# The last block of W_q for two groups, as two blocks of 64 rows on partitions 0 to 63

## The chip, the cores and the metric

The kernel runs on one core of a Trainium2 chip. The metric is the device time of one execution in microseconds (us). Before the change the median of three runs is 735.13 us (734.92 to 736.19). The engines that matter here are TensorE (PE, with its weight loads PEld), VectorE (DVE), ScalarE (ACT), and SyncE (SP), whose queue issues nearly all loads from HBM to on-chip memory. The loads run on the core's 16 DMA engines.

## The reference

Four layers follow each other: attention A, gated MLP B, A again, B again, each with a residual sum, and both A layers use the same weights and caches, as both B layers do. There is one token for each of four batches, `x` of 4 x 640.

```
x = x + A(layernorm(x))          # twice, each followed by
x = x + B(layernorm(x))

A:  q = x @ wq                   # 640 x 4096, 32 heads of 128
    k, v = the last 1024 positions of the caches, for each batch and head
    o = softmax(q k^T / sqrt(128)) v
    out = o @ wo                 # 4096 x 640
B:  gate = x @ W_gate; up = x @ W_up      # 640 x 1728 each
    out = (gate * (gate > 0) * up) @ W_down
```

All values are float32. For four tokens nearly all the work is to bring weights and caches in: each pair of a head and a layer has 4 MB of K and V.

## The kernel before, in words

Nothing is kept of the matrices from one layer to the next, except for the last five heads (the groups `K0` of three and `K1` of two, the row `kept`), whose data stay on chip from layer 0 to layer 1. All else is loaded again.

**Rows in HBM.** The host lays the data out in rows of 128 partitions: `heads` (27 heads in six groups of four and one of three, with their W_q, K, V and W_o in the order in which they are used), `kept` (the same of the last five heads) and `mlp`. A load copies a range of columns of such a row, on all 128 partitions, to a range of columns of `store`, a ring-like buffer of 53,120 columns of four bytes on each partition. One load of 13,312 columns is 6,656 KB.

**W_q.** W_q has 640 rows, which are five blocks (`KC`) of 128 rows. For a group of four heads a block is 512 columns. Its part `q` in the row `heads` is 2,560 columns, five times 512.

**The order of the loads.** `plan` (lines 113 to 191) is a list written at build time: which range of which row goes to which columns of `store`. `put` appends loads cut at given columns, `stretch` (line 124) fills `store` up to its quarters (`QUARTERS`), wraps to column 0 and goes on. `load` (line 196) is called whenever a range of `store` has been used for the last time (`done`, line 220): it takes loads from the plan, in order, for as long as the target columns of the next are free, and issues each with one `nc.sync.dma_start` (line 204) on SP's queue. SP executes them in order; a load whose target is still in use waits on SP, and all later ones wait behind it.

**The compute.** `normalized` (line 289) makes the layer norm, and turns the 640 values of the four tokens into `xT`: on 128 partitions, four columns for each of the five blocks (line 308). `query` (line 329) multiplies blocks 0 to 3 on four column groups of the array into `qp` (line 336), and block 4 on top of the first (line 343), then `query_turned` transposes. `scores` (line 360) multiplies K (line 367), `softmax` and `turned` follow, `values` (line 382) multiplies V (line 395), `project` multiplies W_o (line 425) into the sum `y`. `forward` is the MLP. In `attention` (line 429) these are interleaved over the groups: the query of a group is made two groups ahead, its scores one ahead.

**What sets the order around the change.** The loads go through SP's queue in plan order. The compute waits for each load as a whole: a matmul that needs one column of a load waits until all of that load has landed.

Each load raises a semaphore when it has landed. In the trace all loads use the same eight semaphores (99, 101, 102, 103 and 106 to 109), in turn.

Of the kernel before, what the change touches and what calls it, by code (L numbers as in the profile page):

```python
# [7 lines left out]
F32 = mybir.dt.float32  # L8
# [4 lines left out]
B, D, H, DH, W, F = 4, 640, 32, 128, 1024, 1728  # L13
P = 128
KC = D // P
# [10 lines left out]
KV = 4096  # L26
HEADS = [list(range(h, h + 4)) for h in range(0, 24, 4)] + [[24, 25, 26], [27, 28, 29], [30, 31]]
SIDE = 4
N = len(HEADS)
K0, K1 = N - 2, N - 1  # L30
KEPT = len(HEADS[K0]) + len(HEADS[K1])


def of(what, g):
    return [(what, h) for h in HEADS[g]]


def step(g):
# [5 lines left out]
PARTS = {  # L44
    "heads": [("q", 0), ("q", 1), *of("k", 0)] + [p for g in range(K0) for p in step(g)] + of("o", K0 - 1),
    "kept": [*of("o", K0), *of("o", K1), ("q", K0), ("q", K1), *of("k", K0), *of("k", K1), *of("v", K0), *of("v", K1)],
}


# [12 lines left out]
SPARE = 768  # L62
QUARTERS = [STORE // 4, STORE // 2, STORE // 4 * 3, STORE]
FRONT = KEPT * 2 * (D + KV)
FIRST, MOST = 6976, 16320


def size_of(what, i):
    return len(HEADS[i]) * D if what == "q" else D if what == "o" else KV


def spread(parts):


    at, places, cuts = 0, {}, [0]
    for what, i in parts:
        places[what, i] = at
        size = size_of(what, i)
        step = {"q": size // KC, "k": 512, "v": 512, "o": D}[what]
        cuts += range(at + step, at + size + 1, step)  # L80
        at += size
    return places, at, cuts
# [11 lines left out]
def decode_kernel(ctx: ExitStack, tc: tile.TileContext, x, source, sel, out):  # L94
    nc = tc.nc
    const = ctx.enter_context(tc.tile_pool(name="const", bufs=1))
# [3 lines left out]
    ps_p = ctx.enter_context(tc.tile_pool(name="ps_p", bufs=2, space=bass.MemoryType.PSUM))  # L100
# [5 lines left out]
    store = big.tile([P, STORE], F32, name="store")  # L106
# [8 lines left out]
    def put(layer, row, to, *cuts):  # L115

        for lo, hi in zip(cuts, cuts[1:]):
            assert hi - lo <= MOST and to % 64 == 0 and lo in known[row] and hi in known[row], (row, lo, hi)
            assert to + hi - lo <= (STORE if to < STORE else STORE + SPARE), (row, lo, hi, to)
            plan.append((layer, row, lo, hi, to))  # L120
            to += hi - lo
        return to

    def stretch(layer, lo, end, to, goals):

        while lo < end:
            room = min([g - to for g in goals if g - to >= 2048] or [0])
            hi = max(c for c in ROWS["heads"][2] if c <= min(end, lo + room))
            if hi > lo:
                to = put(layer, "heads", to, lo, hi)  # L130
                lo = hi
            else:
                to = 0
        return to

    def at_part(what, i):
        return WHERE[what, i][1]

    def near(c, row="heads"):

        return max(x for x in ROWS[row][2] if x <= c)
# [37 lines left out]
        lo = hi  # L179
    hi = near(lo + 5120)  # L180
    to = put(1, "heads", to, lo, hi)
    lo, hi = hi, near(hi + STORE - to)
    put(1, "heads", to, lo, hi)
    v = at_part("v", HEADS[K0 - 1][-1])
    to = stretch(1, hi, near(v - 8192), 0, QUARTERS)
    to = put(1, "heads", to, near(v - 8192), heads_end)
    cuts = [0, 7040, 12160, GU0 + 3 * GU, WD1 + WD, MLP - 4 * D, MLP - 2 * D, MLP - D, MLP]
    for lo, hi in zip(cuts, cuts[1:]):
        to = put(1, "mlp", to if to + hi - lo <= STORE else 0, lo, hi)
# [6 lines left out]
    def load():  # L196

        if not held:
            nc.sync.dma_start(out=first_q, in_=source["heads"][:, :HELD])
        while plan and not any(live[plan[-1][4]:plan[-1][4] + plan[-1][3] - plan[-1][2]]):  # L200
            layer, row, lo, hi, to = plan.pop()
            live[to:to + hi - lo] = [True] * (hi - lo)
            held.setdefault((layer, row), []).append((lo, hi - lo, to))
            nc.sync.dma_start(out=place(to, hi - lo), in_=source[row][:, lo:hi])

    def place(to, n):
        return store[:, to:to + n] if to < STORE else probs[:, W - SPARE - 48 + to - STORE:][:, :n]
# [22 lines left out]
    def part(layer, what, h, lo, n):  # L230

        row, first = WHERE[what, h]
        return get(layer, row, first + lo, n)

    def part_done(layer, what, h, lo, n):
        row, first = WHERE[what, h]
        done(layer, row, first + lo, n)
# [6 lines left out]
    nc.scalar.dma_start(out=sel_sb, in_=sel)  # L244


    xT = const.tile([P, KC * B + 28], F32, name="xT")


    qT = const.tile([P, SIDE - 1 + SIDE * SIDE * B], F32, name="qT")  # L250
# [35 lines left out]
            nc.tensor.matmul(m[32 * g:32 * g + 32], sel_q, a, start=True, stop=True, tile_position=(0, 32 * g))  # L286
        return m

    def normalized():

        ysb, xc, sq = probs[:, :QUARTER], gates[:, :QUARTER], gates[:, QUARTER:2 * QUARTER]
        waits[0] = True
        su = small.tile([P, 1], F32, name="su", bufs=1)
        nc.vector.tensor_reduce(su, y, axis=AX.X, op=ALU.add)
        nc.scalar.copy(ysb, y)
        busy(2)
        mu = mean(su, "mu")
        nc.vector.tensor_tensor(xc, ysb, mu.to_broadcast([P, QUARTER]), op=ALU.subtract)
        ss = small.tile([P, 1], F32, name="ss", bufs=1)
        nc.scalar.activation(sq, xc, AF.Square, accum_out=ss)  # L300
        busy(1)

        pt = ps_p.tile([P, KC, 32], F32, tag="p", name="xt_ps")
        nc.tensor.transpose(pt[:, :4], xc[:, :P], ident)
        for g in range(4):
            nc.tensor.matmul(pt[32 * g:32 * g + 32, 4, :B], xc[:, P:], ident[:, 32 * g:32 * g + B],
                             start=True, stop=True, tile_position=(0, 32 * g))
        nc.vector.tensor_copy(xT[:, :KC * B].rearrange("p (c b) -> p c b", b=B), pt[:, :, :B])
        return ss

    def deviation(ss):
        var = mean(ss, "var")
        rs = small.tile([P, 1], F32, name="rstd")
        nc.scalar.activation(rs, var, AF.Sqrt, bias=eps_sb)
        nc.vector.reciprocal(rs, rs)
        return rs
# [12 lines left out]
    def query(layer, g, spread=False):  # L329


        n = len(HEADS[g]) * P
        qp[g] = ps_m.tile([P, n], F32, tag="m", name="qp")
        for c in range(KC - 1):
            for a, b in [(0, HELD - c * n), (HELD - c * n, n)] if g == 0 and c * n < HELD < c * n + n else [(0, n)]:
                nc.tensor.matmul(qp[g][32 * c:32 * c + 32, a:b], xT[:, B * c:B * c + 32],  # L336
                                 part(layer, "q", g, c * n + a, b - a),
                                 start=True, stop=c > 0 and not spread or b < n, tile_position=(0, 32 * c))
        part_done(layer, "q", g, 0, (KC - 1) * n)
        c = KC - 1  # L340
        m = n // 4 if spread else n
        for a in range(n // m):
            nc.tensor.matmul(qp[g][32 * a:32 * a + 32, a * m:a * m + m], xT[:, B * c:B * c + 32],  # L343
                             part(layer, "q", g, c * n + a * m, m), start=False, stop=True, tile_position=(0, 32 * a))
        part_done(layer, "q", g, c * n, n)
# [82 lines left out]

    def attention(layer):
        gs = order[layer]  # L430
        rstd = deviation(normalized())
        table(AF.Exp)
        query(layer, gs[0], True)
        query_out(gs[0], rstd)
        query(layer, gs[1])
        query_turned(gs[0])
        go_on()
        query_out(gs[1], rstd)
        scores(layer, gs[0])
        query(layer, gs[2])  # L440
        softmax(gs[0])
        query_turned(gs[1])
        query_out(gs[2], rstd)
        for before, g, after, then in zip([None] + gs, gs, gs[1:] + [None], gs[2:] + [None] * 2):
            totals(g)
            turned(g)
            if layer == 0 and after is None:
                live[STORE:] = [False] * SPARE
                load()
            if before is not None:  # L450
                values_turned(before)
            if then is not None and before is not None:
                query(layer, then)
                query_out(then, rstd)
            if after is not None:
                scores(layer, after)
                softmax(after)
            else:
                table(AF.Sqrt)
            if then is not None:  # L460
                query_turned(then)

            if before is not None and not (layer == 0 and after is None):
                project(layer, before)
            values(layer, g, after is None)
        values_turned(gs[-1])
        if layer == 0:
            project(layer, gs[-2])
        project(layer, gs[-1], True)
# [134 lines left out]
```

## Time and profile before

| | us |
|---|---|
| median of three runs | 735.13 |
| lowest and highest | 734.92, 736.19 |
| the profiled execution | 734.91 |
| its span, from the first to the last instruction | 733.0 |
| PE busy in the span | 448.8 (61%) |
| DVE busy | 75.3 (10%) |
| ACT busy | 47.1 (6%) |
| bytes read from HBM | 311.85 MB, 426 GB/s over the span |

The profiled execution lies 0.22 us under the median. The mean granted TensorE clock is 0.82. A profile shows each engine's instructions, the DMA queues and what ended each wait. A share of the DMA is a mean over the core's 16 DMA engines: at 1.00 all sixteen move data all the time.

### The profile page before, as it was taken

Reading aid. Unit: us, or ns where it says so; the run is one execution under the profiler, and the core shown is the slowest. Engines: PE = TensorE matmul, PEld = TensorE weight load, DVE = VectorE, ACT = ScalarE, POOL = GpSimd, SP = SyncE. Lnnn points to the kernel's source line nnn. Section 1 sums busy time; section 2 is a strip of 40 time slices with the busy share of each in tenths; the row PEclk is TensorE's granted clock in tenths of the full one; section 3 lists DMA queues with packets and bytes.
Section 4 is the critical chain, followed back from the end, with each engine's and each line's share of the span. In section 5 each row is a group of like instructions: output and inputs, shape, how many; then the busy total and the mean of one; then the engine's idle time right before and its main releaser. Section 6 shows DMA issues by size and latency. Waiting matters only on the chain.

```text
span 733.0 us, 8209 instructions
## 1 busy us (share of the span) xinstructions
PE 448.8 (61%) x3739; PEld 139.2 (19%) x3739; DVE 75.3 (10%) x279; ACT 47.1 (6%) x88; POOL 0.2 (0%) x4
## 2 busy tenths in 40 slices
PE   0666566746457634529778896546666457555576
PEld 0211111111112111203333231101111012111133
DVE  1111000010000101002101221001010010101011
ACT  0200000000000000001201110000000000000100
POOL 0000000000000000000000000000000000000000
PEclk9988868978868767759999999776878778779779
DMA  9999999999999999999999999999999999999996
GB/s 391 447 432 419 436 445 419 446 419 438 440 418 454 422 434 433 427 426 428 419 401 413 432 432 449 434 433 425 443 424 443 433 425 447 428 429 433 423 424 285
DMA packets 14010, 312.45 MB, mean 426 GB/s; under 512 B 1556, under 2 KB 1812, under 8 KB 7192
## 3 DMA queue, kind: packets, MB, share of 16 engines
q1 hardware_dynamic: 13824, 311.84, 99.0%
q8 instruction: 29, 0.48, 0.2%
q10 hardware_dynamic: 152, 0.09, 0.0%
q14 instruction: 5, 0.04, 0.0%
HBM read 311.85 MB, written 0.08 MB: 426 GB/s over the span
## 4 chain that ended last, share of the span: by engine, by line
DMA 55%; PE 29%; another core or an unknown queue 14%; DVE 1%; issue 1%; ACT 0%; SPq 0%; DVEq 0%; ACTq 0%
DMA store<-in_heads 39%; PE ps L367 13%; PE po L395 9%; DMA store<-in_kept 9%; DMA store<-in_mlp 7%; PE y L425 2%; PE pp L380 1%; PE qp L336 1%; PE gu L482 1%; PE qp L343 1%; PE qt L355 1%; DVE nm L371 0%; PE ot L415 0%; ACT probs L375 0%
## 5 line engine op out<-in xcount | busy, mean ns | idle before, releaser
L367 PE MATMUL ps<-store,qT 128*4 128x512 f32 x1024 | 166.2, 715 | 119.8 <-DMA store<-in_heads 98.1
L395 PE MATMUL po<-store,pT 128*16 128x512 f32 x1024 | 154.3, 726 | 99.3 <-DMA store<-in_heads 93.5
L367 PEld LDWEIGHTS ps<-store,qT 128*4 128x4 f32 x1024 | 30.1, 95 | 236.2 <-DMA store<-in_heads 113.9
L395 PEld LDWEIGHTS po<-store,pT 128*16 128x16 f32 x1024 | 32.9, 111 | 206.4 <-issue 123.8
L371 DVE TENSOR_REDUCE nm<-ps 128x1 f32<-128x1024 f32 x18 | 22.0, 1225 | 266.4 <-PE ps L367 266.4
L375 ACT ACTIVATE probs<-ps,nm 128x1024 f32<-128x1024 f32 x18 | 20.1, 1114 | 346.8 <-DVE nm L371 338.7
L425 PE MATMUL y<-store,oT 128*4 128x160 f32 x512 | 24.7, 324 | 17.6 <-DMA store<-in_heads 16.0
L391 DVE COPY pT<-pp 128x16 f32<-128x16 f32 x128 | 17.2, 169 | 141.4 <-PE po L395 141.4
L482 PE MATMUL gu<-store,xT 128*32 128x256 f32 (+1 forms) x288 | 21.5, 362 | 5.5 <-DMA store<-in_mlp 4.8
L402 ACT COPY gates<-po 128x512 f32<-128x512 f32 x16 | 9.4, 587 | 234.8 <-PE po L395 234.8
L336 PE MATMUL qp<-store,xT 128*32 128x512 f32 (+2 forms) x130 | 21.1, 607 | 4.8 <-DMA store<-in_heads 4.7
L380 PE MATMUL pp<-sel_sb,probs 128*128 128x128 f32 x144 | 19.5, 281 | 0.0
L425 PEld LDWEIGHTS y<-store,oT 128*4 128x4 f32 x512 | 12.9, 91 | 27.4 <-DMA store<-in_heads 16.7
L380 PEld LDWEIGHTS pp<-sel_sb,probs 128*128 128x128 f32 x144 | 17.1, 145 | 0.0
L408 DVE RECIPROCAL r<-so 128x16 f32<-128x16 f32 x18 | 4.6, 258 | 112.7 <-PE so L406 112.7
L343 PE MATMUL qp<-store,xT 128*32 128x512 f32 (+4 forms) x46 | 16.1, 498 | 0.0
L270 PE MATMUL y<-probs,sel_sb 4*4 4x160 f32 x8 | 0.7, 445 | 24.9 <-DMA sel_sb<-in_sel 24.9
L348 DVE TENSOR_SCALAR gates<-qp,rstd 128x512 f32<-128x512 f32 (+2 forms) x18 | 12.4, 690 | 23.2 <-PE qp L343 20.3
L355 PE MATMUL qt<-sel_sb,gates 128*128 128x128 f32 x64 | 12.8, 325 | 0.0
L482 PEld LDWEIGHTS gu<-store,xT 128*32 128x32 f32 x288 | 10.0, 109 | 14.5 <-DMA store<-in_mlp 9.0
L513 PE MATMUL y<-store,hT 128*4 128x160 f32 x192 | 9.6, 299 | 4.6 <-DMA store<-in_mlp 4.5
L415 PE MATMUL ot<-sel_sb,gates 128*128 128x128 f32 x72 | 11.5, 279 | 1.2 <-DVE gates L399 1.2
(70 smaller groups left out, 113.8 us busy)
## 6 DMA issues: line engine op xcount, KB each, us to landing
store<-in_heads SPq DMA_DIRECT2D x15, 6656.0 KB, 53.1
store<-in_heads SPq DMA_DIRECT2D x5, 6400.0 KB, 51.6
store<-in_heads SPq DMA_DIRECT2D x2, 6848.0 KB, 48.6
store<-in_heads SPq DMA_DIRECT2D x2, 6592.0 KB, 49.5
store<-in_heads SPq DMA_DIRECT2D x2, 6464.0 KB, 48.5
store<-in_mlp SPq DMA_DIRECT2D x15, 640.0 KB, 6.9
store<-in_kept SPq DMA_DIRECT2D x2, 4096.0 KB, 43.7
store<-in_heads SPq DMA_DIRECT2D x1, 8064.0 KB, 23.4
```

Source lines behind the costliest of these rows:

```text
L336: nc.tensor.matmul(qp[g][32 * c:32 * c + 32, a:b], xT[:, B * c:B * c + 32], part(layer, "q", g, c * n + a, b - a), start=True, stop=c > 0 ...
L343: nc.tensor.matmul(qp[g][32 * a:32 * a + 32, a * m:a * m + m], xT[:, B * c:B * c + 32], part(layer, "q", g, c * n + a * m, m), start=False ...
L348: nc.vector.tensor_scalar(gates[:, :len(HEADS[g]) * P], qp.pop(g), rstd, SCALE, op0=ALU.mult, op1=ALU.mult)
L355: nc.tensor.transpose(qt[:, i], gates[:, i * P:(i + 1) * P], ident)
L367: nc.tensor.matmul(ps[32 * b:32 * b + SIDE, j, :], qT[:, at:at + SIDE], part(layer, "k", h, lo, 512), start=i == 0, stop=i == n - 1, tile_ ...
L371: nc.vector.tensor_reduce(nm[g], ps.rearrange("p j n -> p (j n)"), axis=AX.X, op=ALU.max, negate=True)
L375: nc.scalar.activation(probs, ps.rearrange("p j n -> p (j n)"), AF.Exp, bias=nm.pop(g), accum_out=sums[g])
L380: nc.tensor.transpose(pps[g][c // 4][:, c % 4, :], probs[:, c * P:(c + 1) * P], ident)
L391: nc.vector.tensor_copy(to[:, 4 * j:4 * j + 4], pp[j][:, :, i:P:32])
L395: nc.tensor.matmul(po[32 * a:32 * a + SIDE * B, :], t[:, at:at + SIDE * B], part(layer, "v", h, c * 512, 512), start=i == 0 and c < 4, sto ...
L425: nc.tensor.matmul(y[32 * a:32 * a + B], o[:, i], part(layer, "o", h, a * QUARTER, QUARTER), start=False, stop=last and h == HEADS[g][-1], ...
L482: nc.tensor.matmul(gus[j][32 * g:32 * g + 32, :2 * n], xT[:, B * c:B * c + 32], get(layer, "mlp", lo, 2 * n), start=c == 0, stop=c == KC - ...
```

## The change

For two of the six common groups, 3 and 4, the part `q` has four blocks of 128 rows (2,048 columns) instead of five. The fifth block, 128 rows by 512 columns, goes to a new row `half`: its first 64 rows and its last 64 rows lie side by side on partitions 0 to 63, 1,024 columns wide. The row `half` has 64 rows in HBM.

- **Loads.** A `half` part is fetched by eight loads in a loop, one for each `p` in 0, 1, 2, 3, 32, 33, 34, 35: eight rows `p, p+4, ..., p+28`, 4,096 bytes each, 32 KB for a load. In `store` the part takes 1,024 columns on all partitions as far as the plan's book-keeping goes.
- **Plan.** `stretch` inserts the `half` part of a group ahead of the load that holds the start of the group's `q`. In layer 1 there is also a `put` of columns 0 to 1,024 of the row, which is group 3's part, behind the load of 5,120 columns. `FIRST` falls by 1,024, and the last load of `heads` in layer 1 begins 640 columns earlier by its goal.
- **Compute.** `normalized` has two more small matmuls and a copy in the attention layers: they put the second half of the fifth block's values on partitions 0 to 63, in four more columns of `xT`. `query` multiplies the two half blocks with two matmuls of 64 rows instead of one of 128.

```diff
+HALF = 3, 4
...
-FIRST, MOST = 6976, 16320
+FIRST, MOST = 5952, 16320
...
+        todo = [g for g in HALF if lo <= at_part("q", g) < end]
         while lo < end:
             room = min([g - to for g in goals if g - to >= 2048] or [0])
             hi = max(c for c in ROWS["heads"][2] if c <= min(end, lo + room))
-            if hi > lo:
+            if todo and at_part("q", todo[0]) < hi:
+                a = at_part("half", todo.pop(0))
+                to = put(layer, "half", to, a, a + 1024)
+            elif hi > lo:
...
     to = put(1, "heads", to, lo, hi)
+    to = put(1, "half", to, 0, 1024)
     lo, hi = hi, near(hi + STORE - to)
     put(1, "heads", to, lo, hi)
     v = at_part("v", HEADS[K0 - 1][-1])
-    to = stretch(1, hi, near(v - 8192), 0, QUARTERS)
-    to = put(1, "heads", to, near(v - 8192), heads_end)
+    to = stretch(1, hi, near(v - 8832), 0, QUARTERS)
+    to = put(1, "heads", to, near(v - 8832), heads_end)
...
-            nc.sync.dma_start(out=place(to, hi - lo), in_=source[row][:, lo:hi])
+            if row == "half":
+                for p in *range(4), *range(32, 36):
+                    nc.sync.dma_start(out=store[p:p + 29:4, to:to + hi - lo], in_=source[row][p:p + 29:4, lo:hi])
+            else:
+                nc.sync.dma_start(out=place(to, hi - lo), in_=source[row][:, lo:hi])
...
+        if halves:
+            for g in 0, 1:
+                nc.tensor.matmul(pt[32 * g:32 * g + 32, KC, :B], xc[:, P:], ident[:, 64 + 32 * g:64 + 32 * g + B],
+                                 start=True, stop=True, tile_position=(0, 32 * g))
+            nc.vector.tensor_copy(xT[:64, KC * B:KC * B + B], pt[:64, KC, :B])
...
+        if g in HALF:
+            for a in 0, 1:
+                at = B * (c + a)
+                nc.tensor.matmul(qp[g][32 * a:32 * a + 32], xT[:64, at:at + 32], part(layer, "half", g, a * n, n)[:64],
+                                 start=False, stop=True, tile_position=(0, 32 * a))
...
+        "half": [np.concatenate(np.split(wq[:, KC - 1, heads].reshape(P, -1), 2), axis=1) for heads in HEADS],
```

More of the change, by code (lines that the diff above doesn't have):

```diff
@@ L46 @@
     "kept": [*of("o", K0), *of("o", K1), ("q", K0), ("q", K1), *of("k", K0), *of("k", K1), *of("v", K0), *of("v", K1)],
+    "half": [("half", g) for g in HALF],
 }
@@ L64, with blocks @@
 FRONT = KEPT * 2 * (D + KV)
-FIRST, MOST = 6976, 16320
+FIRST, MOST = 5952, 16320
+def blocks(i):
+    return KC - 1 if i in HALF else KC
 def size_of(what, i):
-    return len(HEADS[i]) * D if what == "q" else D if what == "o" else KV
+    if what in ("q", "half"):
+        return (blocks(i) if what == "q" else 2) * len(HEADS[i]) * P
+    return D if what == "o" else KV
 def spread(parts):
@@ L78, in spread @@
         size = size_of(what, i)
-        step = {"q": size // KC, "k": 512, "v": 512, "o": D}[what]
+        step = {"q": size // blocks(i), "k": 512, "v": 512, "o": D, "half": size}[what]
         cuts += range(at + step, at + size + 1, step)
@@ L244, in decode_kernel @@
     nc.scalar.dma_start(out=sel_sb, in_=sel)
-    xT = const.tile([P, KC * B + 28], F32, name="xT")
+    xT = const.tile([P, (KC + 1) * B + 28], F32, name="xT")
     qT = const.tile([P, SIDE - 1 + SIDE * SIDE * B], F32, name="qT")
@@ L287, in mean, with normalized @@
         return m
-    def normalized():
+    def normalized(halves=False):
         ysb, xc, sq = probs[:, :QUARTER], gates[:, :QUARTER], gates[:, QUARTER:2 * QUARTER]
@@ L301, in normalized @@
         busy(1)
-        pt = ps_p.tile([P, KC, 32], F32, tag="p", name="xt_ps")
+        pt = ps_p.tile([P, KC + 1, 32], F32, tag="p", name="xt_ps")
         nc.tensor.transpose(pt[:, :4], xc[:, :P], ident)
@@ L307, in normalized @@
                              start=True, stop=True, tile_position=(0, 32 * g))
-        nc.vector.tensor_copy(xT[:, :KC * B].rearrange("p (c b) -> p c b", b=B), pt[:, :, :B])
+        nc.vector.tensor_copy(xT[:, :KC * B].rearrange("p (c b) -> p c b", b=B), pt[:, :KC, :B])
+        if halves:
[3 more added lines that the diff above has]
+            nc.vector.tensor_copy(xT[:64, KC * B:KC * B + B], pt[:64, KC, :B])
         return ss
@@ L337, in query @@
                                  part(layer, "q", g, c * n + a, b - a),
-                                 start=True, stop=c > 0 and not spread or b < n, tile_position=(0, 32 * c))
+                                 start=True, stop=c > (g in HALF) and not spread or b < n,
+                                 tile_position=(0, 32 * c))
         part_done(layer, "q", g, 0, (KC - 1) * n)
         c = KC - 1
+        if g in HALF:
[3 more added lines that the diff above has]
+                                 start=False, stop=True, tile_position=(0, 32 * a))
+            part_done(layer, "half", g, 0, 2 * n)
+            return
         m = n // 4 if spread else n
@@ L430, in attention @@
         gs = order[layer]
-        rstd = deviation(normalized())
+        rstd = deviation(normalized(True))
         table(AF.Exp)
@@ L561 @@
     parts = {
-        "q": [wq[:, :, heads].reshape(P, -1) for heads in HEADS],
+        "q": [wq[:, :blocks(i), heads].reshape(P, -1) for i, heads in enumerate(HEADS)],
+        "half": [np.concatenate(np.split(wq[:, KC - 1, heads].reshape(P, -1), 2), axis=1) for heads in HEADS],
         "k": kc.reshape(B, H, 2, 512, DH).transpose(1, 4, 2, 0, 3).reshape(H, P, KV),
@@ L589 @@
         "kept": laid["kept"],
+        "half": laid["half"],
         "mlp": mlp_row,
@@ L596 @@
             for n, a in arrays.items()}
-    source = {n: args[n] for n in ("heads", "kept", "mlp")}
+    source = {n: args[n] for n in ("heads", "kept", "half", "mlp")}
     out = nc.dram_tensor("out_x", (P, QUARTER), F32, kind="ExternalOutput").ap()
```

## The prediction

> **What bounds the kernel now.** I read the page first (DMA queues, costliest groups, issues), then stretches of the span, the end of the chain, and the waits of SP's queue.
>
> ```profile
> span 733.0 us, 8209 instructions
> ...
> q1 hardware_dynamic: 13824, 311.84, 99.0%
> q8 instruction: 29, 0.48, 0.2%
> ...
> L367 PE MATMUL ps<-store,qT 128*4 128x512 f32 x1024 | 166.2, 715 | 119.8 <-DMA store<-in_heads 98.1
> ...
> store<-in_heads SPq DMA_DIRECT2D x15, 6656.0 KB, 53.1
> ```
>
> The queue of the loads fills 99.0% of sixteen DMA engines' span; TensorE's largest group, the scores, waits 119.8 us, 98.1 of them for `in_heads`. So the time is the time of the bytes plus any time in which an engine of the sixteen has nothing to do. A 6,656 KB load lands 53.1 us after its issue. In stretches:
>
> ```profile
> 30.00:58.00 28.00, 20.81 (x149) 5.78 (x141) 4.00 (x7) 1.62 (x4) 0.00 (x0) 0.88 1.00 433
> 404.00:720.00 316.00, 203.46 (x1646) 61.59 (x1642) 33.56 (x125) 19.43 (x36) 0.00 (x0) 0.81 1.00 433
> 725.00:726.00 1.00, 0.49 (x9) 0.14 (x1) 0.17 (x1) 0.00 (x0) 0.00 (x0) 1.00 0.72 297
> 726.00:727.00 1.00, 0.77 (x24) 0.63 (x28) 0.00 (x0) 0.00 (x0) 0.00 (x0) 1.00 0.55 223
> 727.00:728.00 1.00, 0.67 (x24) 0.29 (x19) 0.00 (x0) 0.00 (x0) 0.00 (x0) 1.00 0.48 180
> 728.00:729.00 1.00, 0.99 (x24) 0.30 (x16) 0.00 (x0) 0.00 (x0) 0.00 (x0) 1.00 0.28 102
> 729.00:730.00 1.00, 0.44 (x8) 0.11 (x8) 0.00 (x0) 0.00 (x0) 0.00 (x0) 1.00 0.01 3
> ```
>
> The last two columns are the DMA share and GB/s. At full share the rate is 433 GB/s, 27.1 for one engine; a 6,656 KB load takes 6.82 MB / 433 = 15.7 us, so 53.1 us are three to four loads queued. From 725 on some engines have ended while others go on: the shares left are 0.72 + 0.55 + 0.48 + 0.28 + 0.01 = 2.04 us of sixteen engines, so all could have ended near 727.0. The chain's end:
>
> ```profile
> 698.61 30.91 DMA store<-in_mlp
> 729.52 0.04 issue
> 729.56 0.50 PE y L513 x8
> ```
>
> The last load lands at 729.52, 2.5 us behind that mean. Behind it come 0.50 us of TensorE, a copy and the store, so what the last engine gains or loses is the kernel's.
>
> **Eight loads at a time.** SP's issues from 337.0 to 350.5, the first of them in the list of issues, and SP's wait ahead of the last:
>
> ```profile
> 337.03 4.71 SPq L204 DMA_DIRECT2D store<-in_kept  x6
> 347.30 3.36 SPq L204 DMA_DIRECT2D store<-in_mlp  x3
> ...
> store<-in_kept SPq DMA_DIRECT2D x1, 2048.0 KB, 13.3
> ...
> SPq L204 <- DMA store<-in_kept: 2.2, 1, 2.2
> ```
>
> Nine loads. The ninth ends at 347.30 + 3.36 = 350.66 and an issue takes 0.33, so it starts at 350.33: SP has waited 2.2 us, to the moment at which the first lands (337.03 + 13.3). A load takes the semaphore of the eighth before it and waits on SP until that one has landed; SP holds back everything behind it.
>
> **The change part by part.**
>
> *Where the loads go.* A `half` part is eight loads in one go. By the cuts of the plan: q of group 3 begins at column 2,560 + 2,560 + 16,384 (q0, q1, k0) + 35,328 (step 0) = 56,832. In layer 0 `stretch` puts part 3 ahead of the load that holds this column, and part 4 later: two bursts. In layer 1 the loads run to 44,544 in `store` column 39,552; the new `put` takes 1,024, so the next load reaches up to `near`(44,544 + 53,120 - 40,576 = 57,088), which is 56,832, a cut. `stretch` then starts exactly at 56,832, and `lo <= at_part("q", 3)` holds: part 3 is loaded again. Three bursts in layer 1, five in all, 40 loads of 32 KB; part 3's second copy in layer 1 is 256 KB that nobody needs, 0.26 MB / 433 = 0.6 us.
>
> *What a burst does to the queue.* The burst's eighth load waits for the load just ahead of the burst, since that holds its semaphore. This load is at the tail of the queue, so when it has landed on its last engine, everything large has. The next large load stands behind the eighth on SP. So each burst drains the queue: the engines run dry, SP issues the eighth, then the next large load, and only then do sixteen engines start again. Behind SP's wait stand the large loads, and behind them TensorE.
>
> Its price, from these rows (the first load of the kernel, the store at the end, two issues in a row):
>
> ```profile
> first_q<-in_heads SPq DMA_DIRECT2D x1, 896.0 KB, 4.6
> ...
> out_x<-probs SPq DMA_DIRECT2D x1, 80.0 KB, 1.6
> ...
> 340.46 0.33 SPq L204
> ...
> 340.83 0.43 SPq L204
> ```
>
> - One issue more on SP: the two start 0.37 apart, the second takes 0.43. I take 0.4 us.
> - Starting an empty queue: the first load takes 4.6 us, of which 0.92 MB / 433 = 2.1 are transfer, 2.5 us of start; the store 1.6 less 0.2, 1.4 us. Below this nothing speaks for less. I take 2.0, between them: the load is the same kind of thing, but stands at a cold start.
> - The last engine. Instruction fetches take 0.2% of sixteen spans of 733 us, 23.5 us in 29 packets of 16 KB, 0.8 us each, and a packet takes one engine. A drain waits for the last of sixteen: at least 0.8 us behind the mean, at most two of them on one engine, 1.6, where a drain comes 15 to 60 us after another point at which the engines were even. I take 1.2, the middle.
> - Seven loads are in the queue in the meantime. If eight rows go to eight engines, these have 7 x 4,096 bytes / 27.1 = 1.06 us to do, the others nothing: minus 0.5 in the mean, between 0 and 1.06.
>
> Sum for one burst: 0.4 + 2.0 + 1.2 - 0.5 = 3.1 us; lower end 0.4 + 1.4 + 0.8 - 1.06 = 1.5, upper end 0.4 + 2.5 + 1.6 - 0 = 4.5. Five: 15.5 (7.7 to 22.5).
>
> *The end.* A drain sets all engines even, so less of the 2.5 us is left at the end: minus 1.0 (0 to 1.5).
>
> *Bytes moved between engines.* The fifth block's bytes leave the upper partitions. Hidden in the drains, which set the engines even; without the drains it is the first rival.
>
> *TensorE and the rest.*
>
> ```profile
> L343 PE MATMUL qp<-store,xT 128*32 128x512 f32 (+4 forms) x46 | 16.1, 498 | 0.0
> ...
> L308 DVE COPY xT<-xt_ps x4: 179/179/179, 27.7 to 711.5; 128x20 f32<-128x20 f32 x4
> ```
>
> Four queries have one matmul more, 4 x 0.5 = 2 us, beside TensorE's waits above. `normalized` has two small matmuls and a second copy of 0.18 us in each attention layer, and every query matmul reads 32 columns of `xT`, the new four among them, so it waits for that copy: about 0.5 us at 27.7 and at the start of layer 1, covered by loads already queued; uncovered 1.0. SP has 40 issues more, 17 us, in which it would have waited for room anyway. The `half` parts waste 512 columns of 53,120 each, 1% of the room, against 53.1 us of queued loads; uncovered 0.6 us of lead each. The later start of the last large load lies ahead of 30.91 us of MLP loads. All zero.
>
> **The sum.** 15.5 + 0.6 - 1.0 = 15.1 us on the profiled execution's 734.91 (span 733.0), which is 0.22 under the median of 735.13. I say 750.0 us. With every bound at its end at once: 734.91 + 7.7 + 0.6 - 1.5 = 741.7 and 734.91 + 22.5 + 0.6 + 0 = 758.0.
>
> **The rivals.**
>
> *Even engines.* If the restart were cheap, the shift of bytes would decide. Eight engines would carry 16 KB more for each of four parts and 32 KB for the spare one, 96 KB or 3.6 us; the other eight 64 KB less, 2.4 us. If those relieved are the late ones, the best end is the mean, 727.0 + 0.6 = 727.6 instead of 729.52: 733.0 us, faster by 0.26%. For it: the shares after 725, with about half of the engines done by 727. Against it: the ninth load's wait at 350.33. It decides if a burst costs under 1.9 / 5 = 0.4 us, less than the one issue. [...] No row of this profile names an engine.
>
> *Wrong engines.* The same, with the late ones loaded more: 729.52 + 3.6, 738.5 us.
>
> *The eight loads one after the other.* They write the same columns of `store` on interleaved rows (p, p + 4, ...). If the framework takes their ranges as overlapping, each waits until the one before has landed: 40 x (1.4 to 2.5) = 56 to 100 us; with the drains' lag and issues, about 820 us. For it: SP does wait for the landing of earlier loads,
>
> ```profile
> SPq L204 <- DMA store<-in_heads: 290.2, 31, 22.3
> ```
>
> against it: their partitions differ. [...]
>
> **How the numbers follow.** Drains 0.80 (750.0 us); even engines 0.10 (733.0, or no change if the spare part eats it); wrong engines 0.03 (738.5); one after the other 0.07 (820). A measurement of this kernel tells some 0.2%, 1.5 us, from no change. Drains, wrong engines and serial loads are slower: 0.90. Even engines I split, 0.05 faster and 0.05 within 0.2%. The likeliest case's own range is 741.7 to 758.0. For 8 in 10 the range takes in the wrong engines below: 738.5 to 758.0, which leaves out 0.10 + 0.07.
>
> **What would show it.** Five stretches in which the DMA share falls toward zero for two to three microseconds: in layer 0 one behind the first 48,640 columns of `heads` (24.9 MB / 433 = 57.5 us and the start, near 61) and one behind 87,040 (near 109), in layer 1 the second some 17 us behind the first (12,288 columns lie between), the third some 32 us behind the second (25,088 columns); right at their start SP issues the eighth `in_half` load on a landing. The list of issues has 40 of `in_half`. The wait of L367 and L395 for `in_heads` grows by about the sum. If the shares stay at 1.00 across the `in_half` issues, the drains are wrong; if SP waits seven times for `in_half` in each burst, the loads run one by one.

## The result, and the profile after

The changed kernel takes 757.08 us in the median of six runs (755.15 to 758.08), the kernel before 735.02 (734.80 to 736.19): a ratio of 1.0292, with a 95% interval of 1.0275 to 1.0308. That is 22.1 us more. The profiled execution took 757.75 us.

From the page of the changed kernel: the span, the GB/s of its 40 slices (18.9 us each), the queue of the loads with packets, MB and share of sixteen engines' span, the largest groups of TensorE with busy time, mean and idle time before them, and the issues of the new row. The line numbers have moved: the scores are now L397, the values L425, a query's blocks 0 to 3 L358.

```profile
span 756.0 us, 8302 instructions
...
PE 459.5 (61%) x3755; PEld 139.5 (18%) x3755; DVE 75.5 (10%) x281; ACT 47.1 (6%) x88; POOL 0.2 (0%) x4
...
GB/s 383 433 454 347 432 344 421 438 448 416 440 434 418 447 421 436 425 433 419 405 380 376 427 430 352 372 408 390 440 434 415 445 428 426 445 430 422 432 419 281
...
q1 hardware_dynamic: 14464, 312.11, 97.2%
...
L397 PE MATMUL ps<-store,qT 128*4 128x512 f32 x1024 | 167.9, 731 | 115.9 <-DMA store<-in_heads 94.1
L425 PE MATMUL po<-store,pT 128*16 128x512 f32 x1024 | 154.5, 733 | 103.0 <-DMA store<-in_heads 96.2
...
L358 PE MATMUL qp<-store,xT 128*32 128x512 f32 (+2 forms) x130 | 21.4, 662 | 14.4 <-DMA store<-in_heads 14.3
...
store<-in_half SPq DMA_DIRECT2D x40, 32.0 KB
```

Two rows give the first reading. Span times share is the time for which packets ran on an engine, and the rest of the span is time without one. Before: 733.0 x 0.990 = 725.7 with packets and 7.3 without. After: 756.0 x 0.972 = 734.8 and 21.2. The share is rounded, which is worth 0.4 us. Summed packet by packet from the traces, the time without packets is 7.0 us before and 21.0 after, and from here on such times are these sums. So 14.0 us of the loss are empty engines, and 8.9 us are packets that took longer, of which only 0.6 are more bytes (312.11 against 311.84 MB).

The empty engines sit where the prediction put them: in the slices of 347, 344, 352, 372 and 390 GB/s. Five windows of 10 us; the last two columns are DMA share and GB/s. First the changed kernel:

```profile
58.00:68.00 10.00, 5.68 (x26) 0.94 (x26) 0.00 (x0) 0.00 (x0) 0.00 (x0) 0.66 0.66 250
107.00:117.00 10.00, 5.01 (x46) 2.06 (x50) 1.68 (x6) 1.21 (x2) 0.00 (x0) 0.54 0.72 269
455.00:465.00 10.00, 7.87 (x71) 1.94 (x63) 2.03 (x8) 1.21 (x2) 0.00 (x0) 1.00 0.78 296
473.00:483.00 10.00, 5.07 (x24) 1.14 (x28) 0.35 (x2) 0.00 (x0) 0.00 (x0) 0.50 0.86 336
506.00:516.00 10.00, 4.91 (x26) 0.84 (x26) 0.00 (x0) 0.00 (x0) 0.00 (x0) 0.83 0.87 340
```

The same windows before the change:

```profile
58.00:68.00 10.00, 6.63 (x30) 1.35 (x30) 0.92 (x1) 0.00 (x0) 0.00 (x0) 0.66 0.96 412
107.00:117.00 10.00, 8.40 (x78) 2.71 (x78) 2.38 (x10) 1.21 (x2) 0.00 (x0) 0.84 0.98 426
455.00:465.00 10.00, 1.21 (x8) 0.37 (x12) 0.00 (x0) 0.00 (x0) 0.00 (x0) 0.50 1.00 435
473.00:483.00 10.00, 5.28 (x29) 1.03 (x31) 1.15 (x3) 0.00 (x0) 0.00 (x0) 0.83 1.01 437
506.00:516.00 10.00, 5.84 (x41) 1.39 (x42) 0.35 (x2) 0.00 (x0) 0.00 (x0) 0.66 1.00 431
```

Two more slices are low, 380 and 376 GB/s (378 to 416 us, the first MLP), but there the engines are busy: the share is 1.01. Compared at equal bytes moved, this trace falls 3.5 us further behind the one before between 345 and 410 us of that one. The trace of run 1 below, whose loads are the same up to there, falls back by 1.1. So up to 2.4 us of this profiled execution come and go between executions, and no run says why.

The chain that ended last runs through two of the five windows, by start, length and what it was (L219 issues a load of eight rows, L221 a large load):

```profile
460.59 17.21 DMA store<-in_heads
477.80 0.02 issue
477.81 0.62 SPq L219
478.44 0.05 issue
478.49 0.02 SPq L221
478.51 0.03 issue
478.54 0.39 SPq L221
478.92 0.04 issue
478.97 32.08 DMA store<-in_heads
511.05 0.02 issue
511.06 0.62 SPq L219
```

A large load lands at 477.80; 0.01 us later SP issues the eighth load of the burst, and after it, at 478.54, the next large load. At 511.05 it repeats. The eighth load had waited for the large load ahead of its burst, and held back the large load behind it.

The loads around the first burst, read from the trace (issue, rows x bytes, row in HBM, landing on the last engine):

```
 2.10  128x59392  in_heads  62.28
 2.87    8x4096   in_half   62.48
 3.69    8x4096   in_half   62.69
...
44.73    8x4096   in_half   63.70
62.29    8x4096   in_half   64.39
63.04  128x47104  in_heads  79.34
```

### The profile page after: what moved, and what is told of

It is laid out like the page before. It is cut to its first block, busy times and chain, and to the rows that moved or that the text cites. A ratio compares the mean times of both kernels' runs of the same rounds, so it can differ in the third digit from the quotient of the medians.

```text
span 756.0 us, 8302 instructions
## 1 busy us (share of the span) xinstructions
PE 459.5 (61%) x3755; PEld 139.5 (18%) x3755; DVE 75.5 (10%) x281; ACT 47.1 (6%) x88; POOL 0.2 (0%) x4
## 3 DMA queue, kind: packets, MB, share of 16 engines
q1 hardware_dynamic: 14464, 312.11, 97.2%
HBM read 312.11 MB, written 0.08 MB: 413 GB/s over the span
## 4 chain that ended last, share of the span: by engine, by line
DMA 78%; PE 16%; another core or an unknown queue 4%; issue 1%; DVE 1%; SPq 0%; ACT 0%; ACTq 0%; DVEq 0%
DMA store<-in_heads 61%; DMA store<-in_kept 8%; DMA store<-in_mlp 8%; PE ps L397 8%; PE po L425 4%; PE qp L358 1%; PE y L543 1%; PE y L455 1%; PE gu L512 1%; PE pp L410 1%; PE qp L373 1%; PE po L294 0%; ACT probs L405 0%; PE qt L385 0%
## 5 line engine op out<-in xcount | busy, mean ns | idle before, releaser
L397 PE MATMUL ps<-store,qT 128*4 128x512 f32 x1024 | 167.9, 731 | 115.9 <-DMA store<-in_heads 94.1
L425 PE MATMUL po<-store,pT 128*16 128x512 f32 x1024 | 154.5, 733 | 103.0 <-DMA store<-in_heads 96.2
L397 PEld LDWEIGHTS ps<-store,qT 128*4 128x4 f32 x1024 | 29.9, 96 | 238.3 <-DMA store<-in_heads 109.3
L425 PEld LDWEIGHTS po<-store,pT 128*16 128x16 f32 x1024 | 33.2, 113 | 211.4 <-issue 138.1
L358 PE MATMUL qp<-store,xT 128*32 128x512 f32 (+2 forms) x130 | 21.4, 662 | 14.4 <-DMA store<-in_heads 14.3
L410 PEld LDWEIGHTS pp<-sel_sb,probs 128*128 128x128 f32 x144 | 17.1, 146 | 0.0
L373 PE MATMUL qp<-store,xT 128*32 128x512 f32 (+4 forms) x38 | 12.6, 494 | 5.2 <-DMA store<-in_heads 5.2
```

The source lines that it names most:

```text
L397: nc.tensor.matmul(ps[32 * b:32 * b + SIDE, j, :], qT[:, at:at + SIDE], part(layer, "k", h, lo, 512), start=i == 0, stop=i == n - 1, tile_ ...
L410: nc.tensor.transpose(pps[g][c // 4][:, c % 4, :], probs[:, c * P:(c + 1) * P], ident)
L425: nc.tensor.matmul(po[32 * a:32 * a + SIDE * B, :], t[:, at:at + SIDE * B], part(layer, "v", h, c * 512, 512), start=i == 0 and c < 4, sto ...
```

## The experiments

All times below are medians. The kernel before, on the same chip as each, has 734.80 us beside runs 1 to 4 and 734.81 beside the others.

**1. Without the second copy of part 3.** Four bursts instead of five, and 0.27 MB less.

```diff
-        todo = [g for g in HALF if lo <= at_part("q", g) < end]
+        todo = [g for g in HALF if lo < at_part("q", g) < end]
```

> The changed kernel without the second copy of part 3 in layer 1: four bursts of eight loads instead of five. Drain theory: the whole +22.1 us of the change is five drains of about 4.4 us, so one less gives 757.1 - 4.4 = 752.7 us (751.5 to 754). Rival, the narrow loads cost time by their number or bytes wherever they stand: 32 loads for 40 take a fifth off as well, 752.7; this run alone does not tell the two apart, it gives the price of one burst and the base for the next three. Third theory, the compute side (second copy, more matmuls) costs the time: no change, 757.

753.31 us, ratio 1.0248 (1.0230 to 1.0267): 3.8 less than the changed kernel, for one burst and the copy, as far as medians of four and six runs tell. The next three runs start from this kernel.

**2 and 3. The large load ahead of the last of the eight.** Seven narrow loads, the large load, then the eighth; and six, the large load, then two. Bytes, engines and number of loads are those of run 1.

```diff
-                for p in *range(4), *range(32, 36):
+                parts_of = [*range(4), *range(32, 36)]
+                for p in parts_of[:7]:            # run 3: [:6], and [6:] below
                     nc.sync.dma_start(out=store[p:p + 29:4, to:to + hi - lo], in_=source[row][p:p + 29:4, lo:hi])
+                rest.extend((p, to, lo, hi) for p in parts_of[7:])
             else:
                 nc.sync.dma_start(out=place(to, hi - lo), in_=source[row][:, lo:hi])
+                while rest:
...
```

> As e1, but of each burst seven loads go out, then the next large load, then the eighth. The large load still is the eighth behind the one ahead of the burst, so it still waits for that to land and the queue still drains; only one narrow issue (0.67 us in the changed kernel's trace) goes from in between. Drain theory: four drains, each 0.7 us shorter, e1 minus 2.7, about 750 us. Rival by number of narrow loads: as e1.

> As e1, but six loads go out, then the next large load, then the last two: the same loads, bytes and engines, one place earlier than in e2. The large load now waits for the load before the one ahead of the burst, and is queued while that one still runs: no drain. Drain theory: 735 plus at most 2.4 us for the bytes that went to eight of the engines, 735 to 738 us. Rival by number of narrow loads: as e1, about 752.

With seven ahead: 753.93 us, ratio 1.0256 (1.0235 to 1.0278), no gain over run 1: the large load is now the eighth, and waits itself. With six ahead: 740.83 us, ratio 1.0075 (1.0060 to 1.0090). One place in the queue takes 12.5 us off run 1, 3.1 for each of four bursts. That is still 2.8 above the 738 that was expected at most; runs 7 and 9 take it up. The page rows of runs 1 and 3:

```profile
span 752.0 us, 8294 instructions
...
q1 hardware_dynamic: 14336, 311.84, 97.3%
```

```profile
span 738.2 us, 8294 instructions
...
q1 hardware_dynamic: 14336, 311.84, 98.9%
```

Time without packets falls from 20.2 to 8.4 us, against 7.0 before the change. So the drain is shown, by the same loads without it. Run 2 was also to tell the price of the eighth load's own issue, 2.7 us for four; its median shows nothing of it, but its trace does in part. In three of the four drains the empty time is shorter than in run 1, by 0.75 to 0.9 us (3.15 to 2.4, 3.2 to 2.4, 3.2 to 2.3). In the other one it is 0.6 longer, and 1.5 us more are empty in the first MLP, where no burst stands. Why is not known.

**4. One load of 64 rows for each part.** No burst at all, sixteen engines again: in the trace such a load raises its semaphore in sixteen steps, a load of eight rows in one right behind its issue and eight at its landing.

```diff
-                for p in *range(4), *range(32, 36):
-                    nc.sync.dma_start(out=store[p:p + 29:4, to:to + hi - lo], in_=source[row][p:p + 29:4, lo:hi])
+                nc.sync.dma_start(out=store[:64, to:to + hi - lo], in_=source[row][:, lo:hi])
```

> As e1, but each part comes by one load of 64 rows instead of eight loads of eight rows. The compute is the changed kernel's. Drain theory: no drain, and 64 rows share out over sixteen engines, so the bytes are even: 735 us (734.3 to 736). If the bytes on eight engines cost something, e3 lies above this one by it (up to 2.4 us); if they even out late engines, below. Compute theory: still near 750 us.

747.28 us, ratio 1.0162 (1.0143 to 1.0181): a miss by 12 us, without drains. Run 8 takes it up.

**5 and 6. Tiny loads in the kernel before.** Its own loads and compute, and at four places eight loads of eight rows by 32 bytes into an unused tile (the four places are listed in `BURSTS`): all eight ahead of a large load, or six ahead of it and two behind.

```diff
+            rows_of = [*range(4), *range(32, 36)] if (layer, row, lo) in BURSTS else []
+            for p in rows_of[:8]:                 # run 6: [:6]
+                nc.sync.dma_start(out=pad[p:p + 29:4], in_=source["heads"][p:p + 29:4, :8])
             nc.sync.dma_start(out=place(to, hi - lo), in_=source[row][:, lo:hi])
+            for p in rows_of[8:]:                 # run 6: [6:]
+                nc.sync.dma_start(out=pad[p:p + 29:4], in_=source["heads"][p:p + 29:4, :8])
```

> The kernel before, with its own loads and compute, and at four places in the order of the loads (ahead of the loads that begin at columns 47,616 and 87,040 of the heads in layer 0, and at 44,544 and 83,968 in layer 1) eight loads of eight rows by 32 bytes each into an unused corner of the memory. 1 KB in all at each place: no bytes to speak of, no shift between engines, no change in the compute. If a group of eight loads in a row drains the queue at 3.1 us each, as the first four runs give it: 734.8 + 4 x 3.1 = 747.2 us, perhaps 1 less because the end then finds the engines more even. If the drain needs the 32 KB of each load, or the shift of bytes or the compute makes the loss: 734.8 to 736.

> The same tiny loads at the same four places, but six ahead of the large load and two behind it, so that the large load is in the queue before the load ahead of the group has landed. If it is the drain that costs and not the number of loads: 734.8 to 736 us. If each small load costs by itself (issue, start, 32 loads at 0.3 us or more): 745 or above. With the loads of 32 KB in this same order the time was 740.8; if this run stays near 735, the 6 us of that run are its bytes on eight engines or its compute, not its loads' number or place.

Eight: 754.62 us, ratio 1.0266 (1.0246 to 1.0286). Six and two: 737.48 us, ratio 1.0033 (1.0016 to 1.0049). Four groups of loads that carry 2 KB each (8 loads of 8 rows by 32 bytes; the expectation's 1 KB was a slip) cost 17.1 us by their place alone. Their rows, eight first:

```profile
span 750.5 us, 8243 instructions
...
q1 hardware_dynamic: 14336, 311.85, 97.1%
```

```profile
span 734.5 us, 8242 instructions
...
q1 hardware_dynamic: 14336, 311.85, 99.0%
```

Without packets: 21.4 against 7.0 us, 3.6 for each group, where run 1 has (20.2 - 7.0) / 4 = 3.3: tiny loads leave the gap emptier than narrow ones. Both kinds of drain have slower packets behind them too: the first sixteen large packets take 0.6 to 0.8 us longer than such packets do elsewhere; why is not shown. The two profiled executions differ by 16.0 us, 14.0 of it empty time and 2.0 slower packets, 4.0 for each group. The medians give 4.3; the profiled execution of run 5 was its fastest, and the rest isn't explained.

The 32 loads by themselves leave 2.7 us (run 6), 0.08 for each: neither nothing nor the 0.3 that a price for each load would have made.

**7. The changed compute alone**, on the loads of before.

```diff
-    xT = const.tile([P, KC * B + 28], F32, name="xT")
+    xT = const.tile([P, (KC + 1) * B + 28], F32, name="xT")
...
+        if g in HALF:
+            for a in 0, 1:
+                rows = slice(64 * a, 64 * a + 64)
+                nc.tensor.matmul(qp[g][32 * a:32 * a + 32], xT[rows, B * c:B * c + 32], part(layer, "q", g, c * n, n)[rows],
+                                 start=False, stop=True, tile_position=(64 * a, 32 * a))
```

> The loads of the kernel before, unchanged, and the changed compute alone: two matmuls of 64 rows in place of one of 128 for two groups, two more small matmuls and a copy in the layer norm. The prediction put all of this at zero: 735 us (0 to +1). If the 6 us that remain without drains come from the compute: about 740.

738.97 us, ratio 1.0058 (1.0043 to 1.0073): 4.2 us for what the prediction put at zero. No load of this kernel was changed, but its page says that the loads are slower:

```profile
span 737.9 us, 8243 instructions
...
q1 hardware_dynamic: 13824, 311.84, 98.9%
```

Packets took 729.5 us, 3.4 more than before, for the same packets and bytes; the time without them is 8.4, 1.4 more. The four columns of `xT` make the tile 208 bytes on a partition instead of 192, and all that lies behind it moves, `store` from byte 9,472 to 9,504.

**8. One load of 64 rows, to every second partition.** As run 4, but partitions 0, 2, ... 126. The half matmuls multiply two other blocks of W_q again in place of the fifth, so the kernel leaves the fifth block out for groups 3 and 4.

```diff
-                nc.sync.dma_start(out=store[:64, to:to + hi - lo], in_=source[row][:, lo:hi])
+                nc.sync.dma_start(out=store[::2, to:to + hi - lo], in_=source[row][:, lo:hi])
```

> Each half part is fetched by one load of 64 rows, as in the run with one load for each part (747.3 us), but to every second partition (0, 2, ... 126) instead of partitions 0 to 63. The two half matmuls multiply two other blocks of W_q again in place of the fifth block, so this part of the query is changed; the work and its times stay the same. If that run's 12 us come from sixteen engines writing to one half of the partitions at a time: 735 to 737 us. If a 64-row load in the middle of the large ones costs as such: about 747.

739.32 us, ratio 1.0059 (1.0042 to 1.0076): 8.0 less than run 4, and the same as run 7, which has nearly the same compute and the same place of `store`. The windows at the fourth of these loads (500.27 to 506.13 in run 4, 495.25 to 498.60 in run 8, first landing to last), run 4 first:

```profile
500.00:506.00 6.00, 1.18 (x8) 0.26 (x12) 0.00 (x0) 0.00 (x0) 0.00 (x0) 0.68 0.94 311
```

```profile
495.00:499.00 4.00, 0.98 (x8) 0.26 (x12) 0.00 (x0) 0.00 (x0) 0.00 (x0) 0.79 1.02 439
```

The engines are as busy in both, but move 311 against 439 GB/s. (The view counts a packet where it starts, which is how a share can pass 1.00; counted where the packets run, both shares are 1.00 to 1.01.) In run 4 the 64 packets of 4,096 bytes of this load take 237 ns in the mean, those of 49,152 beside them 2,363; in run 8 160 and 1,817. So a 64-row load cost nothing as such that runs 8 and 7 can tell (739.32 against 738.97). What differs between the loads of runs 4 and 8 is the partitions that they write: with partitions 0 to 63 alone, this load's packets took 77 ns longer, and those of the large load beside it 546 ns. Why is not shown.

**9 and 10. The place of `store` alone**, in the kernel before, by the unused tile ahead of it.

```diff
-    big.tile([P, 8], F32, name="pad")
+    big.tile([P, 16], F32, name="pad")            # run 10: [P, 24]
```

> The kernel before with one edit: the unused tile ahead of the buffer store has 16 columns instead of 8, so store begins at byte 9,504 of each partition (64 x 148.5) instead of 9,472 (64 x 148). The changed compute moves store in just this way, since xT has four columns more. If the place of store is what costs 4.2 us in the run with the changed compute alone: 739 us, packets of 53,248 bytes taking 1,969 ns in the median instead of 1,966. If it is the changed compute itself: 734.8.

> The kernel before with 24 columns of that unused tile: store begins at byte 9,536 (64 x 149). If what costs is a start that is no multiple of 64 bytes: 734.8 us, as before, with packets of 53,248 bytes at 1,966 ns. If any move of store costs, or if a multiple of 128 or 256 is wanted (9,472 is 37 x 256): about 739.

`put` lets every load begin at a multiple of 64 columns of `store`, which is 256 bytes, so each load's place moves with `store`. At 9,504: 738.43 us, ratio 1.0049 (1.0034 to 1.0064). At 9,536: 737.67 us, ratio 1.0038 (1.0024 to 1.0052). So 3.6 of the 4.2 us of run 7 are the place, and 9,536, which is 149 x 64, cost 2.9 as well, against the first theory of run 10. Run 9's rows:

```profile
span 736.3 us, 8209 instructions
...
q1 hardware_dynamic: 13824, 311.84, 99.0%
```

Packets: 728.9 us, 2.8 more; time without them 7.4, 0.4 more. Each packet pays a little. The median ns by size, from the traces:

```
bytes in a packet   before (9,472)  run 9 (9,504)  run 10 (9,536)  changed (9,504)  run 11 (9,472)
 5120                    196             200            199             200              196
20480                    761             765            764             765              761
53248                   1966            1969           1968            1968             1966
```

3.5 ns or so on each of 13,824 / 16 = 864 packets of an engine are 3.0 us.

**11 and 12. `store` back at byte 9,472**, in the changed kernel and in the kernel of run 3, by leaving the unused tile out.

```diff
-    big.tile([P, 8], F32, name="pad")
```

> The changed kernel without the unused tile, so that store begins at byte 9,472 again; nothing else differs. If the place of store adds to the drains: 757.1 - 4.2 = 752.9 us. If the drains, which wait for the last engine anyway, hide it: 756 to 757.

> Six narrow loads, then the large load, then two (740.8 us), without the unused tile, so that store begins at byte 9,472 again. With the place of store worth 4.2 us: 736.6 us, and what is left to 734.8 is the shift of 16 KB to each of eight engines at four places together with the 32 small loads (2.4 us more than the mean on an engine for 64 KB, by 27.1 GB/s, if the late ones get it). If the 6 us of that run were the bytes alone: 740.8.

The changed kernel: 754.12 us, ratio 1.0264 (1.0246 to 1.0282), 3.0 less. The other: 737.53 us, ratio 1.0041 (1.0026 to 1.0057), 3.3 less. Their rows:

```profile
span 754.1 us, 8302 instructions
...
q1 hardware_dynamic: 14464, 312.11, 97.1%
```

```profile
span 735.0 us, 8294 instructions
...
q1 hardware_dynamic: 14336, 311.84, 98.9%
```

Run 12 moves four parts' bytes to eight engines and takes 737.53; run 6 moves none and takes 737.48. Run 12 also has the changed compute and the rest of the changed plan, which run 6 has not. So neither these nor the shift of bytes cost anything that the two runs can tell, whose times scatter over 2.6 and 2.7 us.

**The ladder.** From the changed kernel down: 757.08; `store` back, 754.12 (-3.0); no drains and no second copy, 737.53 (-16.6); the kernel before, 734.81 (-2.7, which run 6 has too, with tiny loads and without the changed compute). No kernel that was run beats the one before.

## Why the prediction was right, and where not

It said 750.0 us, slower, and 757.08 came, inside its range of 738.5 to 758.0. The mechanism was right and the sum was 7 us short: the ladder has 3.0 for the place of `store` and 2.7 that small loads alone also cost (run 6), both put at nothing, and 16.6 where the prediction had 15.1. That the time still lies in the range, 0.9 us under its top, is in part luck: the top was made of drains at their dearest, and the drains came out near the middle.

**The bursts: right, in number, place and price.** Five, 40 loads; the drains at 62.3, 112.0, 459.9, 477.8 and 511.1 us, where 61, 109, and then 17 and 32 us behind each other were said (17.9 and 33.3). The price of 3.1 is what runs 1 and 3 give; the step of 16.6 us, less 0.6 for the copy, gives 3.2 for each of five. Its terms were less right than their sum. One issue more on SP was 0.4 and is 63.04 - 62.29 = 0.75: the issue of an eight-row load takes 0.62 us (the chain above), the large ones took 0.33 to 0.43. Starting an empty queue was 2.0; in all five drains the first packets of the large load begin 1.0 us behind the start of its issue. Together, behind the landing, it is 1.7 us of empty engines in each drain where 2.4 were put. The last engine's lag was 1.2, less 0.5 for the work of the seven loads; in the first three drains 1.1 to 1.4 us of engine time lie empty ahead of the landing, in the last two 0.3 and 0.4, 0.9 in the mean. And 0.6 to 0.8 us of slower packets follow each restart, which the prediction had not. The three make 3.3.

**The second copy: right in kind.** Run 1 takes off 3.8 us; with 3.2 for its burst, 0.6 is left for the copy, as said. This difference is smaller than the scatter of the runs.

**The end, minus 1.0: it came to 0.1.** The windows of the changed kernel at its end:

```profile
746.00:748.00 2.00, 1.70 (x41) 0.89 (x33) 0.17 (x1) 0.00 (x0) 0.00 (x0) 1.00 1.00 411
748.00:750.00 2.00, 1.27 (x32) 0.75 (x32) 0.00 (x0) 0.00 (x0) 0.00 (x0) 1.00 0.81 312
750.00:751.00 1.00, 0.00 (x0) 0.00 (x0) 0.00 (x0) 0.00 (x0) 0.00 (x0) 1.00 0.35 125
751.00:752.00 1.00, 0.86 (x24) 0.47 (x24) 0.00 (x0) 0.00 (x0) 0.00 (x0) 1.00 0.07 28
```

The mean end is 748 + 1.62 + 0.35 + 0.07 = 750.0 and the last landing 752.47, 2.4 us behind it, where it was 2.5. The last drain is 240 us ahead of the end; by then the engines have drifted apart again.

**"TensorE and the rest ... All zero": the step that failed.** The prediction looked for work in the added matmuls and the copy, and for waits. They cost about 0.5 us (run 7 less run 9, which were on different chips). What it passed over is a size: the four columns of `xT` move `store` by 32 bytes, and every load into it pays, 3.0 us here, 3.6 alone. 9,472 is 37 x 256, and 9,504 and 9,536 are multiples neither of 256 nor of 128, so the three places don't tell if either multiple is what counts. The price doesn't grow with the distance: 64 bytes on it was 2.9 us, less than the 3.6 for 32. Why a place costs is not shown.

The zero for SP's "40 issues more, 17 us, in which it would have waited for room anyway" failed in the small: 32 such loads without drains cost 2.7 us (runs 6 and 12). Whether it is the issues or the loads themselves, and where this time goes, isn't settled. In run 6's trace the large loads land within 0.4 us of before through layer 0, where half of the tiny ones are; a lag that stays grows to 1 us between 388 and 407 us, where there are none.

**"Bytes moved between engines": zero, and no cost shows**, even without the drains that were to hide it (runs 12 and 6, to about 1 us).

**What would show it.** The waits of the scores and the values for `in_heads` were to grow by about the sum. They didn't. The rows of the page of before that the prediction didn't show:

```profile
PE 448.8 (61%) x3739; PEld 139.2 (19%) x3739; DVE 75.3 (10%) x279; ACT 47.1 (6%) x88; POOL 0.2 (0%) x4
...
L395 PE MATMUL po<-store,pT 128*16 128x512 f32 x1024 | 154.3, 726 | 99.3 <-DMA store<-in_heads 93.5
...
L336 PE MATMUL qp<-store,xT 128*32 128x512 f32 (+2 forms) x130 | 21.1, 607 | 4.8 <-DMA store<-in_heads 4.7
```

Scores and values wait 94.1 + 96.2 us for `in_heads` against 98.1 + 93.5. The query waits 9.6 us more (14.3 against 4.7). Over all its lines TensorE waits 221.8 us for `in_heads` against 212.3, 9.5 more, and it was busy for 10.7 us more (459.5 against 448.8), at a mean granted clock of 0.813 against 0.82. So the loss is spread over waits and busy time of several lines, and no two lines show it; the share of the queue does.

**The rivals.** Even engines and wrong engines needed a shift of bytes that counts, by 1.9 to 3.6 us, and run 12 against run 6 shows none. The loads one after the other: the trace has the first two narrow loads issued 0.8 us apart (2.87 and 3.69), long before the first has landed on its last engine (62.48). And 32 tiny loads on interleaved rows cost 0.08 us each in run 6, amid large loads, where this rival had 1.4 to 2.5.

## What to carry to other kernels

The loads on SP's queue take eight semaphores in turn here, so eight small ones in a row ahead of a large one emptied the engines and cost 3.1 us each time (runs 1 and 3) or 4.3 (runs 5 and 6); put the large one in as the seventh (run 3). When a small tile grows, look at where the buffer behind it starts: a move of `store` from byte 9,472 to 9,504 cost this kernel, whose loads fill 99.0% of the span, 0.5% (run 9), one to 9,536 0.4% (run 10). And count the loss on the resource that bounds (span times share, and what is left), not in another engine's waits.

## What the hardware showed that was not expected

- With a load of 64 rows to partitions 0 to 63 in flight, its packets and those of the large load beside it took longer than with one to every second partition: packets of 4,096 bytes 237 ns instead of 160, of 49,152 bytes 2,363 instead of 1,817, and 2.0 us for each 256 KB load (run 4 less run 8, over four). Why is not shown.
- `store` at byte 9,504 or 9,536 instead of 9,472: 2 to 4 ns more in the median packet, of 5 KB or of 53 KB (runs 9 and 10).
- The issue of a load of eight rows held SP for 0.62 us in the median, that of a 128-row load for 0.33 (both in the changed kernel), that of a 64-row load, which runs 4 and 8 have, for 0.48.
- A group of eight tiny loads ahead of a large one cost as much as a burst that carries 256 KB, or more: 4.3 us (runs 5 and 6) against 3.1 (runs 1 and 3).
